# Scores for three pairs at a time in six PSUM banks, two accumulator banks that change hands by halves, and an earlier load of the second batch's v

## The chip, the cores and the metric

The kernel runs on one core of a Trainium2 chip. The metric is the time of one execution on the device, in microseconds (us); the time before is the median of three runs.

## The reference

Attention without softmax, multiplied by `u`, feeds a mixture of experts with one expert per token and a fixed capacity. `u` and `v` are 8 x 3072 x 256, `z` is 8 x 3072 x 64, there are 8 experts with 1024 hidden units, and the capacity is 768 tokens per expert.

```python
scores = (1 / S) * matmul(z, z.T)               # per batch, z is query and key
x = u * matmul(maximum(scores, 0) ** 2, v)      # flattened to tokens
expert = argmax(x @ w_gate); gate = softmax(x @ w_gate)[expert]
disp[e, pos] = x[i]                             # in order of tokens, while pos < capacity
y = maximum(disp @ w1, 0) @ w2
out[i] = gate[i] * y[expert[i], pos[i]]         # 0 for tokens over capacity
```

## The kernel before

Every operand of a matmul is split in a high and a low f16 half, and three products (high-high, high-low, low-high) are added in PSUM. Since experts fill up, the kernel computes attention for the first 14 blocks of 512 tokens only, and goes on in a part that is skipped unless some expert is not full.

**Attention.** A block of 512 queries meets 3072 keys as 12 pairs of 128-key tiles. For each pair, `team` makes scores on TensorE in 64-row matmuls, two side by side in the array (the two key tiles of the pair), 12 instructions for a team of two pairs; each pair takes two banks of the PSUM tag `sc`. `follow` then queues, for each pair, two ReLUs and a square on ScalarE and two passes on VectorE that make the f16 halves in a buffer with the tag `hl`. The main loop multiplies a pair by v: for each of four query tiles `c` six 128-row matmuls, 24 for a pair. The sums of a block stay in two banks of the tag `acc` (`c` = 0, 1 in one, 2, 3 in the other) over all 12 pairs, until `drain` multiplies a bank by `u` on VectorE. Scores are symmetric, so a block makes only part of its pairs: others are transposed out of DRAM (`kept`, loaded as `ld`) or straight from the block before (`nx`, and `corner` for one pair). The 14 blocks make 106 pairs, in 53 teams.

**Banks.** PSUM has eight banks: four for `sc`, three for `acc`, one for `m`, which holds the small products (router logits `lg`, running counts `cum`, and `fps`).

**Order.** The program's order is written by a planner: `op` keeps a model clock for each engine, a `Chain` is a list of steps that wait for engines, `weave` emits what fits beside the matmuls, and `need` moves the model clock of TensorE on until a step is there. Chains of lower rank go first; rank -1 are the followers of scores, -2 the drains. `scores_to(p + 3)` makes a team when the main loop is three pairs ahead of the team's first pair. `calm` keeps chains of rank above 0 off ScalarE and VectorE around the end of a block.

**Around it.** `prepare` loads and splits z and v of a batch of six blocks; for the second batch it is called at pair 12, and all its loads go through the queue of SyncE (SP), where kept blocks, transposes and u go too. `route` (GpSimd scatters its rows to DRAM) and then `ffn`, run for the 8 experts one after the other, follow. In `ffn` the hidden products use `sc` with four banks, the outputs `acc` with three.

Of the kernel before, what the change touches and what calls it, by code (L numbers as in the profile page):

```python
# [20 lines left out]
MROW = 8  # L21
BIG = 1 << 21
# [4 lines left out]
def attention_moe_kernel(ctx: ExitStack, tc: tile.TileContext, u, v, z, w_gate, w1, w2, out, cap):  # L27
# [148 lines left out]
    calm = [False]  # L176
    DMAROOM = 1.2
    chains = []
    done = {}
    small = [False]  # L180

# [19 lines left out]
    class Chain:  # L201
# [38 lines left out]
        def fits(self):  # L240
# [4 lines left out]
            if any(small[0] if k == "small" else k not in done or it[0] == "PE" and done[k] + 3.0 > now for k in it[4:]):  # L245
                return False
# [3 lines left out]
            if eng in ("ACT", "DVE"):  # L250
# [5 lines left out]
                if self.rank < 0:  # L256
                    return self.rank < -1 or ("pair", 3) in done or t - now <= 0.2
# [34 lines left out]
    def init_disp():  # L292
# [13 lines left out]
        def put():  # L306
# [4 lines left out]
              4, clk["PE"] + 1.0, gate="consts")  # L311
# [22 lines left out]
    def prepare(bt, first=False, swap=()):  # L334
# [12 lines left out]

        def ld_z(i):
            def f():
                if i == 0:  # L350
                    bt.zraw = sb.tile([P, JT, DQ], F32, tag="zraw", name="zraw", bufs=1)
                    bt.vm = sm.tile([P, NV + 2], F32, tag="vm", name="vm")
                    if first:
                        nc.vector.memset(bt.vm[:, NM:NM + 1], 2.0 ** -112)
# [7 lines left out]
        def ld_v(i):  # L362
            def f():
                t = sb.tile([P, 4, D], F32, tag="raw", name="vraw", bufs=6)
                nc.sync.dma_start(out=t, in_=vr[:, 4 * i:4 * i + 4, :])  # L365
                bt.vraw[i] = t
            return f
# [29 lines left out]
        def z_group(g):  # L397
# [15 lines left out]
            def tr():  # L413
                if g < 2:
                    st.tp = [ps.tile([P, 4, P], F16, tag="sc", name="ztp", bufs=4) for r in range(2)]
                else:
                    t = ps.tile([P, 2, 4, P], F16, tag="m", name="ztp", bufs=1)
# [4 lines left out]

            left = [2]

            def ev(r):
                def f():
# [3 lines left out]
                    left[0] -= 1  # L430
                    if g >= 2:
                        small[0] = left[0] > 0
# [3 lines left out]
                    [("PE", 0.45, tr, None) if g < 2 else ("PE", 0.45, tr, None, "small")],  # L436
# [122 lines left out]
        if not first:  # L559
            for i in range(zparts):  # L560
                Chain([[("SP", 4.4, ld_z(i), None)]] + norm(i), 1, slow=20.0)
            for i in range(NV):
                Chain([[("SP", 1.46, ld_v(i), None)], [mark(i)]], 2, slow=20.0)
# [15 lines left out]
        if not first:  # L579
# [3 lines left out]
                         lambda: Chain([[("DVE", 0.4, factor, key("f"))]], 3, max(done[key("v", 0)], done["gate"]))))  # L583
# [89 lines left out]
    def route(x, bt, after, lag, cc, rid, follows=(), ahead=(), snapped=()):  # L673
# [31 lines left out]
        def r_lg():  # L705
            st.lg = ps.tile([P, cc, 2, E], F32, tag="m", name="lg", bufs=1)
# [21 lines left out]
        def r_cum():  # L728
            st.cum = ps.tile([P, cc, E], F32, tag="m", name="cum", bufs=1)
# [57 lines left out]
        def tr(h):  # L787
# [8 lines left out]
            [("PE", 0.15, r_lg, None, "small")],  # L796
            [("DVE", 1.1, free(r_arg), None)],
            [("PE", 0.05, r_cum, None, "small") + follows, ("DVE", 0.1, r_dexp, None)],
# [5 lines left out]
    def counts(c=cnt):  # L804
        t = ps.tile([P, E], F32, tag="m", name="fps", bufs=1)
# [44 lines left out]
    def attention(blocks, hook):  # L850
# [3 lines left out]
        bank, held = [0], {}  # L854
        rids = []
# [46 lines left out]
        teams = deque(tuple(computed[i:i + 2]) for i in range(0, len(computed), 2))  # L902
        assert all(len(t) == 2 and t[1] == t[0] + 1 and t[0] % 2 == 0 for t in teams)
# [15 lines left out]
        def team(ps_):  # L919
# [3 lines left out]
            n, g = at(ps_[0])  # L923
            bt, ib, c0, cc = blocks[n]
            t = need(bt.key("z", 2 * g // 4), bt.key("z", ib))
            made = []
            for p in ps_:
                if place[p] >= 2:
                    t = max(t, need((aid, "r", place[p] - 2)))
# [3 lines left out]
                s = [ps.tile([P, BLK], F32, tag="sc", name="sc", bufs=4) for _ in range(2)]  # L933
# [5 lines left out]
                t = op("PE", 0.1 + 3 * w / 2400, t)  # L939
# [3 lines left out]
        def follow(p, s, w, t):  # L943
# [17 lines left out]
            def hi():  # L961
                hl = sb.tile([P, 2, nt, 2, HB], F16, tag="hl", name="hl", bufs=5)
# [29 lines left out]
            def keep():  # L992
# [4 lines left out]

            st = [[("ACT", 0.05 + w * 0.00084, relu(0), None), ("ACT", 0.05 + w * 0.00084, relu(1), (aid, "r", k))],
                  [("ACT", 0.09 + w * 0.00168, square, (aid, "s", k))],
                  [("DVE", 0.07 + w * 0.00107, hi, None, bt.key("vs")), ("DVE", 0.29 + w * 0.0021, lo, (aid, "a", p))]]  # L1000
# [6 lines left out]
            return Chain(st, -1, t, gate=(aid, "s", k - 1) if k else None, hold=HOLD)  # L1007

        def scores_to(p):
            while teams and teams[0][0] - (2 if cornered(teams[0][1]) and blocks[teams[0][0] // NPAIR][1] else 0) <= p:  # L1010
                team(teams.popleft())

# [34 lines left out]
        for p in range(NP):  # L1047
            n, g = at(p)
            bt, ib, c0, cc = blocks[n]
            hook(p)  # L1050
            done.setdefault(("pair", p), clk["PE"])
            loads_to(p + 4)
            i = p % NPAIR
            if i == 0:
                acc[n] = {}
            calm[0] = p < NP - 1 and (i == NPAIR - 1 or i == 0 and n > 0)
            if i == NPAIR // 2:
                ld_u(n)
            for c in range(cc):
                if c % (cc // 2) == 0:  # L1060
                    scores_to(p + 3 if p > 3 else p + 2 if p or c else 0)
                    weave()
# [379 lines left out]
```

## Time and profile before

| | us |
|---|---|
| median of three runs | 787.63 (786.09 to 788.51) |
| the profiled execution | 781.93 |
| its span, from first to last instruction | 780.2 |
| TensorE busy | 770.2 (99%) |
| VectorE busy | 515.7 (66%) |
| ScalarE busy | 400.9 (51%) |
| GpSimd busy | 120.4 (15%) |
| attention on TensorE | until 521.9 |
| experts on TensorE | from 521.9 to the end |

The profile is of one execution. A group of matmuls that overlap in the array is busy as a whole, so a busy TensorE says only that no gap was seen; whether the array streamed at its full rate is read from how many matmuls start in a stretch of time. A wait is put down to the engine or the transfer whose semaphore came last.

### The profile page before, as it was taken

Reading aid. Unit: us, or ns where it says so; the run is one execution under the profiler, and the core shown is the slowest. Engines: PE = TensorE matmul, PEld = TensorE weight load, DVE = VectorE, ACT = ScalarE, POOL = GpSimd, SP = SyncE. Lnnn points to the kernel's source line nnn. Section 1 sums busy time; section 2 is a strip of 40 time slices with the busy share of each in tenths; the row PEclk is TensorE's granted clock in tenths of the full one; section 3 lists DMA queues with packets and bytes.
Section 4 is the critical chain, followed back from the end, with each engine's and each line's share of the span. In section 5 each row is a group of like instructions: output and inputs, shape, how many; then the busy total and the mean of one; then the engine's idle time right before and its main releaser. Section 6 shows DMA issues by size and latency. Waiting matters only on the chain.

```text
span 780.2 us, 16284 instructions
## 1 busy us (share of the span) xinstructions
PE 770.2 (99%) x6474; PEld 569.7 (73%) x6474; DVE 515.7 (66%) x1134; ACT 400.9 (51%) x690; POOL 120.4 (15%) x122
## 2 busy tenths in 40 slices
PE   9999999999999999999999999999999999999996
PEld 3787878888887777878888877876666666666664
DVE  7996888853517789974553259889476575575741
ACT  6966545533206646663431048675455564464541
POOL 0000102020202010210202020202421321313202
PEclk9999999999999999999999999999999999999999
DMA  7659999999988949999969959970698945845001
GB/s 223 142 198 192 256 204 233 203 222 174 185 155 179 286 153 189 225 197 224 204 146 190 180 155 229 338 178 22 206 301 297 332 137 223 285 127 186 28 15 45
DMA packets 283830, 149.49 MB, mean 192 GB/s; under 512 B 229741, under 2 KB 255674, under 8 KB 283744
## 3 DMA queue, kind: packets, MB, share of 16 engines
q1 hardware_dynamic: 278848, 135.57, 71.7%
q0 software_dynamic: 4896, 12.79, 4.8%
q8 instruction: 52, 0.85, 0.5%
q14 instruction: 34, 0.28, 0.1%
HBM read 36.25 MB, written 59.92 MB: 123 GB/s over the span
## 4 chain that ended last, share of the span: by engine, by line
PE 84%; issue 5%; DMA 3%; DVE 2%; SPq 2%; POOL 2%; ACT 1%; POOLq 0%; ACTq 0%; DVEq 0%
PE acc L1083 52%; PE hps L1224 12%; PE yps L1248 11%; PE sc L937 8%; POOL out L84 1%; DMA vraw<-in_v 1%; DMA ld<-kept 1%; DMA wraw<-in_moe_w 1%; SPq L910 1%; PE lg L709 1%; SPq L365 1%; ACT a L959 0%; DVE hl L972 0%; DVE hh L1210 0%; DVE wt L1151 0%
## 5 line engine op out<-in xcount | busy, mean ns | idle before, releaser
L1083 PE MATMUL acc<-v,hl 128*128 128x256 f16 x2280 | 261.2, 273 | 0.2 <-DVE v L520 0.2
L1083 PEld LDWEIGHTS <-hl 128*128 128x128 f16 x2280 | 219.6, 98 | 34.7 <-issue 5.4
L954 ACT ACTIVATE r<-sc 128x512 f32<-128x512 f32 (+1 forms) x212 | 105.5, 550 | 164.8 <-PE sc L937 163.1
L1224 PE MATMUL hps<-fxt,wt 128*128 128x384 f16 (+2 forms) x816 | 127.5, 317 | 0.5 <-DVE hh L1210 0.5
L1248 PE MATMUL yps<-wt,hh 128*128 128x256 f16 (+1 forms) x776 | 126.6, 324 | 0.0
L972 DVE TENSOR_TENSOR hl<-a,hl 128x1024 f16<-128x1024 f32 (+1 forms) x106 | 118.2, 1115 | 3.6
L84 POOL DMA_INDIRECT disp<-xr,slot x54 | 60.6, 1122 | 378.2 <-issue 134.0
L1224 PEld LDWEIGHTS <-wt 128*128 128x128 f16 x816 | 77.5, 98 | 47.8 <-issue 0.9
L1248 PEld LDWEIGHTS <-hh 128*128 128x128 f16 x776 | 75.6, 98 | 48.6
L1083 PE MATMUL acc<-v,ld 128*128 128x256 f16 x960 | 109.2, 273 | 1.2 <-DMA ld<-kept 1.2
L959 ACT ACTIVATE a<-r 128x1024 f32<-128x1024 f32 (+1 forms) x106 | 102.6, 968 | 2.2
L1083 PEld LDWEIGHTS <-ld 128*128 128x128 f16 x960 | 93.0, 98 | 12.7 <-DMA ld<-kept 1.5
L963 DVE CAST hl<-a 128x1024 f16<-128x1024 f32 (+1 forms) x106 | 67.8, 639 | 50.0 <-ACT a L959 49.4
L1210 DVE SCALAR_TENSOR_TENSOR hh<-hps,hh 128x384 f16<-128x384 f32 (+2 forms) x136 | 70.7, 531 | 33.9 <-ACT hh L1209 33.4
L1209 ACT ACTIVATE hh<-hps 128x384 f16<-128x384 f32 (+2 forms) x136 | 63.4, 471 | 50.5 <-PE hps L1224 49.3
L84 POOL DMA_INDIRECT out<-ys,sid x48 | 53.3, 1111 | 126.5 <-DVE ys L1257 74.5
L937 PE MATMUL sc<-zz 64*128 64x512 f16 (+1 forms) x636 | 71.4, 356 | 0.4 <-DVE zz L427 0.2
L1254 ACT ACTIVATE ys<-yps,sg 128x256 f32<-128x256 f32 x48 | 22.6, 472 | 72.6 <-PE yps L1248 68.2
L1083 PE MATMUL acc<-v,nx 128*128 128x256 f16 x504 | 58.5, 273 | 0.0
L1257 DVE SCALAR_TENSOR_TENSOR ys<-yps,sg,ys 128x256 f32<-128x256 f32 x47 | 22.6, 483 | 51.9 <-ACT ys L1254 51.4
L1083 PEld LDWEIGHTS <-nx 128*128 128x128 f16 x504 | 48.4, 98 | 8.3 <-issue 2.8
L691 ACT ACTIVATE xr<-x,rsr 128x256 f16<-128x256 f32 x54 | 24.8, 501 | 55.4 <-DVE rsr L60 51.8
(135 smaller groups left out, 485.1 us busy)
## 6 DMA issues: line engine op xcount, KB each, us to landing
out<-zero SPq DMA_DIRECT2D x48, 512.0 KB, 9.0
kept<-hl SPq DMA_DIRECT2D x40, 512.0 KB, 4.8
wraw<-in_moe_w SPq DMA_DIRECT2D x32, 512.0 KB, 6.1
vraw<-in_v SPq DMA_DIRECT2D x18, 512.0 KB, 6.4
u<-in_u SPq DMA_DIRECT2D x13, 512.0 KB, 5.7
zraw<-in_z SPq DMA_DIRECT2D x2, 768.0 KB, 6.3
zz<-zz SPq DMA_DIRECT2D x4, 384.0 KB, 4.6
xt<-xr SPq DMA_TRANSPOSE x54, 2.5
```

The lines of the kernel that those rows point to most:

```text
L84: r = nc.gpsimd.indirect_dma_start(out=dst, out_offset=bass.IndirectOffsetOnAxis(ap=idx, axis=0), in_=src, in_offset=None, bounds_check=bo ...
L691: return lambda: nc.scalar.activation(st.x16[:, c, 0:D], st.x[:, c, :], AF.Copy, scale=st.rs[:, c:c + 1])
L937: nc.tensor.matmul(s[jj][:, 0:w], lhsT=bt.zz[rows, (kl + jj) % 2, j * P:(j + 1) * P], rhs=bt.zz[rows, (ql + jj) % 2, q0:q0 + w], start=(i ...
L954: nc.scalar.activation(sct[p][:, jj, :], s[jj][:, 0:w], AF.Relu)
L959: nc.scalar.activation(sq[p], sct.pop(p), AF.Square)
L963: nc.vector.tensor_copy(hl[:, :, :, 0, :], sq[p].rearrange("p j (t k) -> p j t k", k=HB))
L972: nc.vector.tensor_sub(hl[:, :, :, 1, :], a.rearrange("p j (t k) -> p j t k", k=HB), hl[:, :, :, 0, :])
L1083: nc.tensor.matmul(o, lhsT=a(h, jj, c), rhs=bt.v2[:, j, l], start=(i + jj + h + l + c % 2 == 0), stop=(i == NPAIR - 1 and jj + h == 2), sk ...
L1209: Chain([[("ACT", 0.05 + w * 0.00083, lambda: nc.scalar.activation(th, src, AF.Relu), None)], [("DVE", 0.07 + w * 0.00104, lambda: nc.vect ...
L1210: [("DVE", 0.07 + w * 0.00104, lambda: nc.vector.scalar_tensor_tensor(out=tl, in0=src, scalar=0.0, in1=th, op0=ALU.max, op1=ALU.subtract), ...
L1224: nc.tensor.matmul(o, lhsT=wx.w1[:, d, wp, f * P:(f + 1) * P], rhs=sx.xt[:, xp * DC + d, a:a + w], start=(q == 0), stop=(q == len(seq) - 1))
L1248: nc.tensor.matmul(y[:, 0 if end else l], lhsT=hid(i, f)[:, sl], rhs=w[:, l], start=(f + i == 0 and l != 1), stop=(f == FC - 1 and i == 1) ...
```

## The change

- Teams of the opening (the first six pairs) stay as they are; all later ones take three computed pairs (`TEAM = 3`), in six `sc` banks. A team may hold pairs on either side of stored pairs or of a block's end.
- The `m` bank is gone: `ztp`, `lg`, `cum` and `fps` take a bank of `sc`. `open_bank` lets a small product in only when the bank it takes has been read, and at least four query tiles before the next team is due; `team` holds TensorE's place in the order until the small product has been read.
- `acc` has two banks. At a block's start and end two pairs are taken together: both for `c` = 0, 1, then both for `c` = 2, 3 (`steps`). `turning` keeps followers of scores from being queued ahead there.
- In `ffn` both kinds of products share the six `sc` banks.
- `hl` has six buffers instead of five, and its VectorE pass is emitted only once the buffer is through (`room_for`); `corner` has a buffer of its own.
- The second batch's v is loaded from pair 3 on, one load for every two pairs, each after the first batch's v in its buffer has been split; z still starts at pair 12.
- The scratch space for dynamic DMA is 8192 instead of the default, and a few ranks and one delay of the third expert's weights change.

```diff
+NHL = 6
+TEAM = 3
-        t = ps.tile([P, BLK], F32, tag="acc", name="warm", bufs=3)
+        t = ps.tile([P, BLK], F32, tag="acc", name="warm", bufs=2)
...
+            if "small" in it[4:] and self.ready + self.lag <= now and not clear[0]():
+                return False
...
-                    return self.rank < -1 or ("pair", 3) in done or t - now <= 0.2
+                    return self.rank < -1 or ("pair", 3) in done and not turning[0] or t - now <= 0.2
...
-                    t = ps.tile([P, 2, 4, P], F16, tag="m", name="ztp", bufs=1)
+                    t = ps.tile([P, 2, 4, P], F16, tag="sc", name="ztp", bufs=6)
...
             for i in range(NV):
-                Chain([[("SP", 1.46, ld_v(i), None)], [mark(i)]], 2, slow=20.0)
+                Chain([[("SP", 1.46, ld_v(i), None) + (held(i) if held else ())],
+                       [mark(i) + ((("pair", NPAIR + 1 + i),) if held else ())]], 2, slow=20.0)
...
-            st.lg = ps.tile([P, cc, 2, E], F32, tag="m", name="lg", bufs=1)
+            st.lg = ps.tile([P, cc, 2, E], F32, tag="sc", name="lg", bufs=6)
...
-        teams = deque(tuple(computed[i:i + 2]) for i in range(0, len(computed), 2))
+        opening = hasattr(blocks[0][0], "to_scores")
+        k = 6 if opening else 0
+        teams = deque(tuple(computed[i:i + 2]) for i in range(0, k, 2))
+        teams.extend(tuple(computed[i:i + TEAM]) for i in range(k, len(computed), TEAM))
...
+            while small[0]:
+                weave()
+                clk["PE"] += 0.1 if small[0] else 0.0
+            latest[:] = [0, *((aid, "r", place[p]) for p in ps_)]
...
-                if place[p] >= 2:
-                    t = max(t, need((aid, "r", place[p] - 2)))
+                if place[p] >= TEAM:
+                    t = max(t, need((aid, "r", place[p] - TEAM)))
-                s = [ps.tile([P, BLK], F32, tag="sc", name="sc", bufs=4) for _ in range(2)]
+                s = [ps.tile([P, BLK], F32, tag="sc", name="sc", bufs=6) for _ in range(2)]
...
-                        corner[n] = sb.tile([P, 4, HB], F16, tag="ld", name="corner", bufs=5)
+                        corner[n] = sb.tile([P, 4, HB], F16, tag="corner", name="corner", bufs=1)
...
+            def room_for():
+                return k < NHL or computed[k - NHL] in through and lines[k - NHL].item() is None
...
+        def open_bank():
+            p, c = where
+            if latest:
+                k = latest[1 + min(latest[0] // 2, len(latest) - 2)]
+                if k not in done or done[k] + HOP > clk["PE"]:
+                    return False
+            if teams and (due() - 3 - p) * CC - c < 4:
+                return False
...
+        def steps():
+            for n, (_, _, _, cc) in enumerate(blocks):
+                i = 0
+                while i < NPAIR:
+                    both = cc == CC and (i == 0 and not (opening and n == 0) or i == NPAIR - 2)
+                    for h in range(2 if both else 1):
+                        for j in range(2 if both else 1):
+                            for c in (2 * h, 2 * h + 1) if both else range(cc):
...
+                                turning[0] = both and (i > 0 or n > 0 and h + j < 2)
+                                yield n * NPAIR + i + j, c
+                    i += 2 if both else 1
...
-                    k = bank[0] - 3
+                k = bank[0] - 2
-                    acc[n][c // 2] = ps.tile([P, 2, D], F32, tag="acc", name="acc", bufs=3)
+                acc[n][c // 2] = ps.tile([P, 2, D], F32, tag="acc", name="acc", bufs=2)
...
-                h = ps.tile([P, BLK], F32, tag="sc", name="hps", bufs=4)
+                h = ps.tile([P, BLK], F32, tag="sc", name="hps", bufs=6)
-            y = ps.tile([P, 2, D], F32, tag="acc", name="yps", bufs=3)
+            y = ps.tile([P, 2, D], F32, tag="sc", name="yps", bufs=6)
...
-            if g == 0 and ib == (b == 0) and b + 1 in bats:
+            if p == 1 and 1 in bats:
+                prepare(bats[1], swap=(("pair", 3 * NPAIR + 3),),
+                        held=lambda i: (b0.key("v", 2 * i + 1), ("pair", 2 * i + 3)))
+            if p == NPAIR and 1 in bats:
+                bats[1].begin_z()
+            if p == b * BPB * NPAIR and b and b + 1 in bats:
                 prepare(bats[b + 1], swap=(("pair", p + 2 * NPAIR + 3),))
...
-    nc = _bacc.Bacc("TRN2", target_bir_lowering=False, num_devices=1)
+    nc = _bacc.Bacc("TRN2", target_bir_lowering=False, num_devices=1, dynamic_dma_scratch_size=8192)
```

## Rows read from the trace of the kernel before

**Rows 1.** The page: busy time and instructions of TensorE, and its 40 slices.

```profile
PE 770.2 (99%) x6474; PEld 569.7 (73%) x6474; DVE 515.7 (66%) x1134; ACT 400.9 (51%) x690; POOL 120.4 (15%) x122
PE   9999999999999999999999999999999999999996
```

**Rows 2.** Waits of TensorE, whole span: us in total, times, longest us.

```profile
PE acc L1083 <- DMA ld<-kept: 1.2, 1, 1.2
PE warm L151 <- DVE ones L121: 1.1, 1, 1.1
PE hps L1224 <- DVE hh L1210: 0.5, 2, 0.4
```

**Rows 3.** Chain that ended last, pieces in order: start us, us, what.

```profile
107.22 1.40 PE sc L937 x12
108.62 5.34 PE acc L1083 x48
113.96 1.40 PE sc L937 x12
...
127.98 1.08 PE sc L937 x12
129.06 15.83 PE acc L1083 x144
...
309.20 2.64 PE acc L1083 x24
...
511.19 0.76 PE sc L937 x12
```

**Rows 4.** Timeline of TensorE, 95 to 110 us, around the one wait for a transfer.

```profile
101.80 2.79 PE L1083 MATMUL acc<-v,ld 128*128 128x256 f16 x24 [1.22 <-DMA ld<-kept]
```

**Rows 5.** Timeline of the SP queue, 80 to 102 us: start us, us of issue.

```profile
84.35 0.53 SPq L365 DMA_DIRECT2D vraw<-in_v  x1
...
86.67 6.25 SPq L910 DMA_TRANSPOSE ld<-kept  x1
92.96 0.58 SPq L365 DMA_DIRECT2D vraw<-in_v  x1
93.58 4.52 SPq L910 DMA_TRANSPOSE ld<-kept  x1
...
99.56 0.94 SPq L365 DMA_DIRECT2D vraw<-in_v  x1
```

**Rows 6.** Stretches: busy us of each engine, granted clock, DMA share, GB/s.

```profile
30.00:60.00 30.00, 30.00 (x273) 23.45 (x271) 27.18 (x52) 22.34 (x35) 0.35 (x1) 1.00 0.75 205
...
80.00:100.00 20.00, 20.00 (x202) 16.39 (x200) 16.42 (x35) 9.24 (x15) 4.87 (x4) 1.00 1.08 271
```

**Rows 7.** Groups by line and shape, ScalarE and VectorE: busy us, mean ns, idle before.

```profile
L954 ACT ACTIVATE r<-sc 128x512 f32<-128x512 f32 x168 | 91.0, 594 | 159.0 <-PE sc L937 157.9
L959 ACT ACTIVATE a<-r 128x1024 f32<-128x1024 f32 x84 | 88.7, 1056 | 1.6
```

**Rows 8.** Line of the drains: duration min/median/max ns; idle of VectorE before them.

```profile
L1025 DVE TENSOR_TENSOR x<-acc,u x27: 678/692/692, 57.5 to 522.1; 128x512 f32<-128x512 f32 x27
...
  PE acc L1083: 23.2, 19
```

**Rows 9.** Timeline of VectorE, ends of block 5 (241 us) and block 11 (463 us).

```profile
241.25 0.69 DVE L1025 TENSOR_TENSOR x<-acc,u 128x512 f32<-128x512 f32 x1 [3.04 <-PE acc L1083]
241.86 0.69 DVE L963 CAST hl<-a 128x1024 f16<-128x1024 f32 x1
242.58 1.23 DVE L972 TENSOR_TENSOR hl<-a,hl 128x1024 f16<-128x1024 f32 x1
243.72 0.69 DVE L963 CAST hl<-a 128x1024 f16<-128x1024 f32 x1
244.44 1.23 DVE L972 TENSOR_TENSOR hl<-a,hl 128x1024 f16<-128x1024 f32 x1
245.58 0.69 DVE L1025 TENSOR_TENSOR x<-acc,u 128x512 f32<-128x512 f32 x1
...
462.77 0.69 DVE L1025 TENSOR_TENSOR x<-acc,u 128x512 f32<-128x512 f32 x1 [3.04 <-PE acc L1083]
...
467.11 0.68 DVE L1025 TENSOR_TENSOR x<-acc,u 128x512 f32<-128x512 f32 x1
```

**Rows 10.** Timeline of TensorE in the experts, 564 to 580 us.

```profile
566.35 1.50 PE L1224 MATMUL hps<-fxt,wt 128*128 128x128 f16 x24 [0.35 <-DVE hh L1210]
...
576.51 2.11 PE L1224 MATMUL hps<-fxt,wt 128*128 128x384 f16 x12 [0.16 <-DVE hh L1210]
```

**Rows 11.** DMA issues of the whole span: KB each, median us to landing.

```profile
vraw<-in_v SPq DMA_DIRECT2D x18, 512.0 KB, 6.4
...
disp<-xr,slot POOLq DMA_INDIRECT x54, 3.9
```

**Rows 12.** A slice of experts: line's DMA to landing (min/median/max), SP's issue, TensorE's use.

```profile
DMA to landing us min/median/max: 3.2/5.1/11.4
...
552.99 1.19 SPq L1178 DMA_TRANSPOSE fxt<-disp  x1
...
564.49 1.50 PE L1224 MATMUL hps<-fxt,wt 128*128 128x128 f16 x24
```

**Rows 13.** Timeline of GpSimd, 541 to 554 us: the densest run of scatters.

```profile
540.95 1.17 POOL L84 DMA_INDIRECT disp<-xr,slot  x1 [22.70 <-DVE ys L1257]
...
552.73 0.97 POOL L84 DMA_INDIRECT out<-ys,sid  x1 [0.31 <-issue]
```

More of the change, by code (lines that the diff above doesn't have):

```diff
@@ L176, in attention_moe_kernel @@
     calm = [False]
+    turning = [False]
     DMAROOM = 1.2
@@ L180, in attention_moe_kernel @@
     small = [False]
+    clear = [lambda: True]
     def free(fn):
@@ L244, in fits @@
             now = clk["PE"]
-            if any(small[0] if k == "small" else k not in done or it[0] == "PE" and done[k] + 3.0 > now for k in it[4:]):
+            if any(small[0] if k == "small" else not k() if callable(k) else
+                   k not in done or it[0] == "PE" and done[k] + 3.0 > now for k in it[4:]):
+                return False
+            if "small" in it[4:] and self.ready + self.lag <= now and not clear[0]():
                 return False
@@ L332, in batch, with prepare @@
         return bt
-    def prepare(bt, first=False, swap=()):
+    def prepare(bt, first=False, swap=(), held=None):
         zparts = 3 if first else 1
@@ L365, in f @@
                 nc.sync.dma_start(out=t, in_=vr[:, 4 * i:4 * i + 4, :])
+                if not bt.vraw and not first:
+                    new_max()
                 bt.vraw[i] = t
@@ L854, in attention @@
         bank, held = [0], {}
+        where, latest, lines, through = [0, 0], [], {}, set()
         rids = []
@@ L1046, in attention @@
             scores_to(0)
[L1047 removed]
+        clear[0] = open_bank
+        operand = {}
+        for p, c in steps():
+            where[:] = p, c
             n, g = at(p)
             bt, ib, c0, cc = blocks[n]
[L1050 to L1052 removed]
             i = p % NPAIR
[L1054 to L1062, printed above, removed]
[L1063 to L1089 removed]
@@ new lines, in attention @@
+            if c == 0:
+                hook(p)
+                done.setdefault(("pair", p), clk["PE"])
+                loads_to(p + 4)
+                if i == 0:
+                    acc[n] = {}
+                if i == NPAIR // 2:
+                    ld_u(n)
+            if c % (cc // 2) == 0:
+                scores_to(p + 3 if p > 3 else p + 2 if p or c else 0)
+                weave()
+            if c == 0:
+                if is_next(p):
+                    take(p)
+                clk["PE"] = max(clk["PE"], need((aid, "a", p), bt.key("v", g),
+                                                *([(aid, "d", n)] if cornered(p) else [])) + HOP)
+                operand[p] = prs.pop(p)
@@ new lines, in attention @@
+            a = operand[p]
+            if i == 0 and c % 2 == 0:
+                k = bank[0] - 2
+                if k in held:
+                    clk["PE"] = max(clk["PE"], need((aid, "x", *held[k])) + HOP)
+                held[bank[0]] = n, c // 2
+                bank[0] += 1
+                acc[n][c // 2] = ps.tile([P, 2, D], F32, tag="acc", name="acc", bufs=2)
+            o = acc[n][c // 2][:, c % 2]
+            for jj in (0, 1):
+                j = 2 * g + jj
+                for h, l in ((0, 0), (0, 1), (1, 0)):
+                    nc.tensor.matmul(o, lhsT=a(h, jj, c), rhs=bt.v2[:, j, l], start=(i + jj + h + l + c % 2 == 0),
+                                     stop=(i == NPAIR - 1 and jj + h == 2), skip_group_check=True)
+                op("PE", 0.328, 0.0)
+                weave()
@@ L1090, in attention @@
+            if i == NPAIR - 1 and c % 2:
+                drain(n, c // 2)
+            if c == cc - 1:
+                through.add(p)
+                operand.pop(p)
+            if i == NPAIR - 1 and c == cc - 1:
+                calm[0] = False
                 need(bt.key("f"), "init")
@@ L1303, in experts @@
                 wxs[i + 1] = Bag()
-                weights(es[i + 1], wxs[i + 1], gate=((eid, "through", i - 1),) if i else ())
+                weights(es[i + 1], wxs[i + 1], gate=((eid, "through", i - 1),) if i else (), slow=5.0 if i == 1 else 0.0)
             if straight[0] and k > 0:
```

95 lines of the change are left out of this document (42 added, 53 removed).

## The prediction

> **What bounds the kernel now.** I read the page first: TensorE is busy for 770.2 of 780.2 us, and VectorE, the next, for 515.7 [rows 1]. Next come TensorE's waits: the longest is 1.2 us for a stored block, the experts wait 0.5 us in two places for VectorE, and with a start of 1.1 us these are nearly all [rows 2]. So hardly any stall is left to remove; the time is what TensorE issues. A busy array is not yet one that streams at its full rate, so the third view is the chain that ended last, read as a clock. In a stretch without scores, 144 matmuls of 256 columns take 15.83 us, 0.1099 us each [rows 3]. The granted clock is 1.00, the 2.4 GHz level, in every stretch read [rows 6], so no gain can come from the clock either.
>
> The same rows show what a team of scores costs beyond its columns. A team of two pairs, both 512 wide, takes 1.40 us; with one pair of 256 it takes 1.08, and with both at 256 it takes 0.76 [rows 3]. Each halved pair takes off 0.32 us, which is three streams of 256 columns at 0.107 us. Six streams of 512 columns are then 1.28 us, and 0.12 us of each team is a fixed cost. From one team to the next, with 48 matmuls between, it is 113.96 - 107.22 = 6.74 us; 48 x 0.1099 + 1.28 = 6.56, so a team costs 0.18 us in all, partly before and partly after it. I use 0.18 to 0.19. It is paid when the array goes from 128-row to 64-row matmuls and back, once for a team, however many pairs it holds.
>
> **Part by part.**
>
> Teams of three. There are 106 pairs made, 53 teams before. After, the opening keeps 3 teams for 6 pairs, and the other 100 pairs make 33 teams of three and one of one: 37 in all. 16 teams fewer x 0.19 us = -3.0 us (-2.9 by the lower value). All of it lies on TensorE, which ends the time, so nothing hides it. Matmuls, columns and weight loads stay the same.
>
> What a team of three asks of ScalarE: two ReLUs of 0.594 us and a square of 1.056 for a pair [rows 7], 2.24 us, 6.7 us for the team. A team needs all six banks, so the last pair's second ReLU must be done before the next team. It ends some 0.64 + 2 x 2.24 + 1.19 = 6.3 us after the team began (0.64 us are the first pair's columns); the next team begins after 1.92 + 0.19 us of scores and 72 matmuls, 10.0 us after this one. So 3.7 us are left for other work of ScalarE (before: 0.64 + 2.24 + 1.19 = 4.1 of 6.74, 2.6 left). I take 0 for this wait. A pair's halves are needed no sooner than before, since the team still comes three pairs ahead, and the second and third have longer.
>
> Two accumulators. A drain takes 0.69 us, and 19 of 27 ran the moment their bank was complete, with VectorE idle before them [rows 8]. After, the other bank is worked on for 24 matmuls, 2.64 us [rows 3], before a drained bank is wanted. So a drain may start 1.95 us late and cost nothing. With three banks one of the two drains of a block already had just this window, and no wait for it shows [rows 2]; the other had a whole block. At the end of block 5 that other drain started at 245.58, behind two pairs' conversions [rows 9]; its bank was complete 1.32 us (12 matmuls) after the first drain's, at 242.57, so it ended 3.70 us after that. In the new order this would cost 3.70 - 2.64 = 1.06 us. At the end of block 11 the drain ran as late [rows 9]: bank complete at 462.77 + 1.32, drained by 467.79. `turning` lets at most one such pass of VectorE (1.23 us) go ahead of a drain, and that fits in the 1.95. The bounds are 0 and 13 boundaries x 1.06 = 13.8 us; I take 0.8 us, less than one late boundary, because nearly all rows are on the side of on time.
>
> Here a rule stands against the change. The Trainium skill, in Perfetto Trace Analysis, section Matmuls under Optimizing Tensor Performance, wants independent matmul groups to rotate through PSUM banks so that the evacuation of one overlaps the next group. Read strictly, a block's two banks are both its own, no third bank covers the drain, and 26 drains x 0.69 = 17.9 us would lie open. The row of 2.64 us speaks against that reading, since the halves let each bank cover the other; the rule's case is the slower rival below.
>
> The small products (14 `lg`, 14 `cum`) lose their bank. They are admitted after the first ReLUs of a team and at least four query tiles (2.64 us) before the next; the window is some 5 of every 10 us. Their instructions stay the same, and a team waits only if VectorE hasn't read the bank. Bounds: 0, and 28 reads behind one 1.23 us pass, 34 us; I take 0, since VectorE is a third idle and the first reader is at the head of its chain. Delay of the router itself ends in scatters that the experts want only at 522 us; nothing on TensorE waits for them earlier.
>
> The early v. TensorE's one wait for a transfer is at 101.80, 1.22 us, for a stored block [rows 4]. That transfer's issue stood on the SP queue from 93.58 to 98.10, behind another that took 6.25 us and two loads of v [rows 5]. DMA is full there (share 1.08, 271 GB/s), and has room in 30 to 60 us (0.75, 205 GB/s) [rows 6]. A load of v is 512 KB; at 205 to 271 GB/s that is 2.0 to 2.6 us each. The two loads of the rows and one more at 99.56 leave this place, so the stored block comes some 4 to 5 us earlier. It is also wanted earlier: 1.32 us by the new order of the first two pairs, and 0.6 us by the three teams saved until then. 1.22 + 1.32 + 0.6 = 3.1 us, under 4; so the wait should go, -1.2 us, but with little to spare: bounds -1.2 and +1.9. In exchange some five loads, 10 to 13 us of DMA, enter 30 to 68 us; what is queued behind them on SP there are writes of `kept` and transposes for the next block, not wanted before 59 us. The maxima of v stay on VectorE, held to block 1, so VectorE's full start (27 of 30 us [rows 6]) gets no more to do. I take -1.0.
>
> Six banks for the experts. Two waits of 0.35 and 0.16 us are for a hidden bank still read by VectorE [rows 10]; with six banks instead of four both should go: -0.5 us. Outputs come from the same six; a bank is wanted again five products later, far longer than the reads take.
>
> Answers at nothing: six `hl` buffers, a buffer for `corner` (leaves five for stored blocks alone), ranks, and the later third weights take away waits or move work that is off TensorE; `room_for` holds a pass back in the order rather than in VectorE's queue.
>
> The sum: -3.0 - 1.0 - 0.5 + 0.8 = -3.7 us. On the profiled execution's 781.93 us that gives 778.2. That execution is 5.7 us under the median of the runs shown; I carry the difference over unchanged, so 787.63 - 3.7 = 783.9 us, 0.47% faster. A measurement of this kernel can tell about 0.3%, 2.4 us, from no change.
>
> **The rivals.**
>
> What is late before stays late. The drains of blocks 5 and 11 cost 2 x 1.06 = 2.1 us in place of my 0.8, and the stored block is waited for as before, 0 in place of -1.0: -3.0 - 0.5 + 2.1 = -1.4, 786.2 us, no change to be told. For it: the halves put two drains where conversions already stood, and the stored block has less than 1 us to spare by my sum. Against it: `turning`, and the two loads that stood in front of it are gone.
>
> Slower: every boundary waits for its drain. A drain that is queued behind two pairs' conversions, as at block 5 [rows 9], costs 1.06 us; at 13 boundaries 13.8 us. With -4.5 us from the other terms that is 796.9. It decides against the change from 0.35 us a boundary on, and is slower to be told from 0.53. For it: block 5 shows the order; against it: 19 of 27 drains on time.
>
> Fewer scatter slots: the change sets the scratch space of dynamic DMA to 8192 in place of its default. The Trainium skill, in SBUF — State Buffer, section on SBUF size, sets 16 KiB of a partition aside for the descriptor rings of GpSimd's DMAs; by that the rings are halved, and no row here shows how full they get. The densest run is ten scatters between 540.95 and 553.70, one every 1.28 us [rows 13], while a landing takes 3.9 us [rows 11], so three are in the air. If each had to wait for the last, these ten would take 39 us instead of 12.8, 26 more. The experts' slice that follows was issued at 552.99 and first used at 564.49, and its landing takes 5.1 us [rows 12], so 6.4 us are to spare and some 20 would be waited: 787.6 - 3.7 + 20 = 804. Against it: the rings as they are show no wait at three in the air, and room for just one would be a far greater cut than a smaller scratch suggests.
>
> The change doesn't do what it says: teams are made late or the moved loads move the wait to another stored block. Only the saved switches less 1 to 2 us are left, about 786 us; it counts with the first rival.
>
> **How the numbers follow.** The forecast, all terms near their value: 0.60. First rival and the like: 0.24. Late drains everywhere: 0.12. Scatters: 0.04. The forecast's cases lie within 781.5 (-3.0 - 1.2 - 0.5 with no new wait is 782.9, and runs spread by over 1 us) and 785.2. The range goes on through the first rival and a few late boundaries to 789.5; over that lies most of the slower cases, under 781.5 little. Faster by over 0.3%: 0.60; within: 0.26; slower: 0.14.
>
> **What would show it.** After: 38 stretches of `sc` on TensorE instead of 54 (the second team of the opening is in two parts), full ones of 18 matmuls lasting 2.04 us (1.92 + 0.12); no wait for `ld` near 100 us; no wait of `hps` for `hh`. Wrong would be the prediction if TensorE waited for a drain (`x`) or for a ReLU at `sc`, if stretches between teams fell short of 0.110 us a matmul, or if scatters came further apart than 1.28 us in the dense run.

## The result, and the profile after

The changed kernel takes 778.47 us (median of 6 runs, 776.74 to 779.68), the kernel before 787.26 us beside it on the same chip (6 runs, 786.09 to 788.51). The ratio is 0.9886, 95% interval 0.9872 to 0.9900: 8.8 us faster, where 3.7 were forecast, and 3 us under the low end of the range. The profiled execution of after took 778.41 us, span 776.5, so it stands in the middle of its runs. That of before did not, and this turns out to be the point of the case.

TensorE on the page of after, beside [rows 1], and its waits, beside [rows 2] (us in total, times, longest us):

```profile
PE 766.8 (99%) x6474; PEld 572.3 (74%) x6474; DVE 514.4 (66%) x1134; ACT 401.1 (52%) x690; POOL 116.6 (15%) x122
...
PE warm L153 <- DVE ones L123: 1.1, 1, 1.1
PE acc L1141 <- DVE v L527: 0.6, 2, 0.5
PE acc L1141 <- DMA ld<-kept: 0.6, 2, 0.3
PE ztp L433 <- DVE zhl L422: 0.5, 2, 0.3
PE acc L1141 <- DVE wm L1188: 0.3, 1, 0.3
```

No wait for a drain (`x`), none for a ReLU at `sc`, none of `hps` for `hh`. The wait for a stored block has fallen from 1.2 us to two that come to 0.6. Without the start, `warm`, the four kinds of small waits come to 2.0 us; those for `ztp` and `wm` are new beside [rows 2].

The chain of after, pieces in order (start us, us, what), beside [rows 3]:

```profile
32.21 2.05 PE sc L958 x18
34.26 5.35 PE acc L1141 x48
39.61 2.05 PE sc L958 x18
41.66 7.96 PE acc L1141 x72
49.62 1.73 PE sc L958 x18
```

A team of three takes 2.05 us: 1.92 of columns and 0.13. From 39.61 to 49.62 it is 10.01 us for a team and 72 matmuls of 0.1099 us: 10.01 - 7.91 - 1.92 = 0.18 us for the team, as much as a team of two cost. There are 38 stretches of `sc` in the whole trace.

If one sets this trace beside the profile of before that stands in the front, attention is 2.4 us shorter (its last matmul starts at 521.82 and 519.38) and the rest 1.3 us: 3.7 us of span, just what I forecast. But the runs differ by 8.8. So 5 us are not in the trace of before at all, and the first thing to do was to profile that kernel again.

### The profile page after: what moved, and what is told of

It is laid out like the page before. It is cut to its first block, busy times and chain, and to the rows that moved or that the text cites. A ratio compares the mean times of both kernels' runs of the same rounds, so it can differ in the third digit from the quotient of the medians.

```text
span 776.5 us, 16291 instructions
## 1 busy us (share of the span) xinstructions
PE 766.8 (99%) x6474; PEld 572.3 (74%) x6474; DVE 514.4 (66%) x1134; ACT 401.1 (52%) x690; POOL 116.6 (15%) x122
## 4 chain that ended last, share of the span: by engine, by line
PE 88%; issue 3%; DMA 3%; DVE 2%; POOL 1%; SPq 1%; ACT 0%; POOLq 0%; ACTq 0%; DVEq 0%
PE acc L1141 51%; PE hps L1287 14%; PE yps L1311 14%; PE sc L958 8%; DMA ld<-kept 2%; DMA vraw<-in_v 1%; POOL out L86 1%; PE lg L722 1%; DVE hl L993 1%; SPq L375 0%; DVE hl L984 0%; DVE wm L75 0%; DVE xr L707 0%; DVE v L527 0%; SPq L369 0%
## 5 line engine op out<-in xcount | busy, mean ns | idle before, releaser
L86 POOL DMA_INDIRECT disp<-xr,slot x54 | 56.8, 1051 | 359.7 <-issue 215.5
L958 PE MATMUL sc<-zz 64*128 64x512 f16 (+1 forms) x636 | 68.5, 355 | 0.0
```

Of the source, the lines that this page charges most:

```text
L86: r = nc.gpsimd.indirect_dma_start(out=dst, out_offset=bass.IndirectOffsetOnAxis(ap=idx, axis=0), in_=src, in_offset=None, bounds_check=bo ...
L958: nc.tensor.matmul(s[jj][:, 0:w], lhsT=bt.zz[rows, (kl + jj) % 2, j * P:(j + 1) * P], rhs=bt.zz[rows, (ql + jj) % 2, q0:q0 + w], start=(i ...
```

## Experiments

**The kernel before once more** (`ctl`, nothing edited).

> The kernel before, unchanged. Open: its runs take 787.3 us, the profiled execution took 781.93. Theory A (a wait that comes and goes): this profile has a span near 785.5 and TensorE has about 5 us of waits that the first profile has not, most of them for transfers. Theory B (the extra lies outside the span): the span is again 780 and the time 787. Against the kernel before: ratio 1.000 within 0.002.

Its median is 787.98 us beside 788.03 for the same kernel, ratio 0.9999 [0.9985, 1.0012], and its profiled execution took 787.93 us, span 786.1, in the middle of the runs. Theory A is right that a wait is there, and wrong about its kind: it is for VectorE and not for a transfer. Waits of TensorE, then TensorE around the second slice of the experts (640 rows are the first slice, 384 and 128 the second and third):

```profile
PE hps L1224 <- DVE hh L1210: 3.6, 2, 3.5
...
548.28 4.07 PE L1224 MATMUL hps<-fxt,wt 128*128 128x384 f16 x24
555.80 6.80 PE L1224 MATMUL hps<-fxt,wt 128*128 128x384 f16 x24 [3.46 <-DVE hh L1210]
562.44 7.96 PE L1248 MATMUL yps<-wt,hh 128*128 128x512 f16 x48
```

The first 24 matmuls (four banks of hidden values) take 4.07 us, then TensorE waits 3.46 us for a bank, and the next 24 take 6.80. ScalarE, which has to read those banks, shows that VectorE is only the last in a row (idle time before an instruction in brackets):

```profile
546.11 0.47 ACT L1254 ACTIVATE ys<-yps,sg 128x256 f32<-128x256 f32 x1 [2.36 <-PE yps L1248]
551.87 0.47 ACT L1254 ACTIVATE ys<-yps,sg 128x256 f32<-128x256 f32 x1 [5.28 <-PE hps L1224]
554.67 1.64 ACT L1209 ACTIVATE hh<-hps 128x384 f16<-128x384 f32 x4 [2.33 <-remote]
```

The output that ScalarE scales at 551.87 was complete when the first slice's last matmul ended, some 0.2 us after 548.28; the four ReLUs at 554.67 came all at once. So ScalarE sat idle beside finished work for 3.4 of the 5.28 us, and for all of the 2.33. Meanwhile GpSimd issued ten scatters (first and last of the row, 1.28 us apart, 0.30 between them):

```profile
540.33 1.16 POOL L84 DMA_INDIRECT disp<-xr,slot  x1 [22.27 <-DVE ys L1257]
...
552.09 0.97 POOL L84 DMA_INDIRECT out<-ys,sid  x1 [0.30 <-issue]
```

And the windows (length; busy us of PE, PEld, DVE, ACT, POOL; granted clock; DMA share; GB/s):

```profile
552.00:556.00 4.00, 0.54 (x4) 0.20 (x2) 1.29 (x3) 1.67 (x5) 0.97 (x1) 0.82 0.55 116
556.00:562.00 6.00, 6.00 (x22) 2.93 (x21) 2.26 (x5) 1.63 (x4) 0.97 (x1) 0.55 0.97 328
```

After the pause the granted clock is 0.55, near the 1.2 GHz level, so the stall is paid for once more: 24 matmuls take 6.80 us in place of 4.07, 2.7 us. Divided by place, ctl against after, in us of the two traces:

| Part of the span | ctl | after | after - ctl |
|---|---|---|---|
| up to the last matmul of attention | 521.22 | 519.38 | -1.84 |
| from there to the experts' second slice | 27.06 | 26.66 | -0.40 |
| second and third slices | 27.36 | 20.93 | -6.43 |
| from the fourth to the last outputs | 203.06 | 202.71 | -0.35 |
| behind them | 7.4 | 6.8 | -0.6 |

The 6.43 us are the stall and its clock. The last line is no part of the change: it varies from 6.6 to 7.9 us among the traces of this study, whatever the kernel. The first profile of before has 21.42 us in the second and third slices. The first line isn't exact either: in six traces in which the code of attention is that of before, its last matmul starts between 521.00 and 524.76, and in five traces with that of the change between 518.60 and 520.85.

**Are the switches and the moved v worth what I said?** `team2` is the change with teams of two; `vlate` is the change with the second batch's v loaded at pair 12 as before.

```diff
-TEAM = 3
+TEAM = 2
```
```diff
-            if p == 1 and 1 in bats:
-                prepare(bats[1], swap=(("pair", 3 * NPAIR + 3),),
-                        held=lambda i: (b0.key("v", 2 * i + 1), ("pair", 2 * i + 3)))
             if p == NPAIR and 1 in bats:
-                bats[1].begin_z()
+                prepare(bats[1], swap=(("pair", 3 * NPAIR + 3),))
```

> The change with teams of two pairs (TEAM = 2); banks, order by halves, early v and all else as in the change. Theory switches: 16 more teams at 0.19 us, 3.0 us over the change, 781.5 us against 787.3 of before (ratio 0.9926); 54 stretches of sc. Rival (the three-pair team itself frees VectorE or ScalarE from waits): the whole gain of 8.8 us goes, 787.

> The change with the second batch's v loaded from pair 12 on, as before; all else as in the change. Theory early v pays: the stored block near 100 us is waited for again, 1.2 us if the first profile is typical (779.7 us), 5 to 6 us if this is the wait that comes and goes (784). Rival (the early load pays nothing): 778.5, no wait of TensorE for ld near 100 us.

team2: 783.05 us (781.50 to 785.42), ratio 0.9941 [0.9921, 0.9961], 4.6 us over the change's median (4.3 by the two ratios; the two were taken on different occasions), where 3.0 were expected. From the first score to the end of attention its trace has 3.1 us more than that of after, 0.5 of it in more waiting, which leaves 2.6 for the switches; 16 teams x 0.18 are 2.9 us. The other 1.5 us of the medians are not in attention; 0.8 of them stand behind the last outputs, where any two traces differ.

vlate: 786.94 us (784.53 to 790.79), ratio 0.9994 [0.9978, 1.0010]; the whole gain is gone, 8.5 us, more than either value that was expected. TensorE waits for stored blocks twice, and the window behind it shows the clock:

```profile
98.89 1.48 PE L1141 MATMUL acc<-v,ld 128*128 128x256 f16 x12 [1.73 <-DMA ld<-kept]
105.00 6.44 PE L1141 MATMUL acc<-v,ld 128*128 128x256 f16 x36 [4.63 <-DMA ld<-kept]
...
105.00:112.00 7.00, 7.00 (x43) 5.40 (x44) 3.85 (x3) 0.00 (x0) 0.00 (x0) 0.66 0.58 127
```

The SP queue says why: in vlate four loads of v issued from 81.47 on, of which the last two are shown, stand ahead of the first transpose, which is issued at 88.59 for 7.44 us; in after the same place has none.

```profile
85.36 1.42 SPq L375 DMA_DIRECT2D vraw<-in_v  x2
...
88.59 7.44 SPq L926 DMA_TRANSPOSE ld<-kept  x1
...
97.59 4.45 SPq L926 DMA_TRANSPOSE ld<-kept  x1
```

The same two issues in after:

```profile
82.96 5.12 SPq L926 DMA_TRANSPOSE ld<-kept  x1
...
89.27 4.41 SPq L926 DMA_TRANSPOSE ld<-kept  x1
```

So 6.36 us of waiting and about 2.3 us of low clock (36 matmuls in 6.44 us; in team2 36 of the same kind take 4.10) stand against the 8.5 us of the medians.

**The moved v alone** (`vearly`: before, with v of the second batch loaded early and nothing else; the edit is that of the change to `prepare` and its calls, so the lines taken from vlate are put into before).

> The kernel before with the early load of the second batch's v alone. Theory early v pays: 1.2 us (786) by the first profile, 5 to 6 us (782) if the wait for the stored block is what comes and goes. Rival (pays nothing): 787.3, ratio 1.000.

788.92 us (786.73 to 790.42), ratio 1.0013 [1.0000, 1.0025]: worth nothing alone. No wait for a stored block is left, but there isn't always one to lose (with the same attention ctl lists none, scr8 0.9 us and hps6 1.4), and a wait of 1.12 us for a ReLU at 113.95 has come. The edits of this change don't add up: moving v is worth 8.5 us where the new order needs its stored blocks earlier, and 0 where it doesn't.

**What is it in the second slice: the banks, the weights, the scratch?** Three single parts put into before, and one taken out of the change. `hps6` gives hidden products seven banks in before, four of `sc` and three of `acc`; `slow5` delays the third expert's weights; `scr8` halves the scratch; `hps4` is the change with two of its six banks passed over after every four hidden products.

```diff
-                h = ps.tile([P, BLK], F32, tag="sc", name="hps", bufs=4)
+                h = ps.tile([P, BLK], F32, tag="sc" if k % 3 else "acc", name="hps", bufs=4 if k % 3 else 3)
```
```diff
...
-                weights(es[i + 1], wxs[i + 1], gate=((eid, "through", i - 1),) if i else ())
+                weights(es[i + 1], wxs[i + 1], gate=((eid, "through", i - 1),) if i else (), slow=5.0 if i == 1 else 0.0)
```
```diff
-    nc = _bacc.Bacc("TRN2", target_bir_lowering=False, num_devices=1)
+    nc = _bacc.Bacc("TRN2", target_bir_lowering=False, num_devices=1, dynamic_dma_scratch_size=8192)
```
```diff
+                if k % 4 == 1 and k > 1:
+                    for _ in range(2):
+                        ps.tile([P, BLK], F32, tag="sc", name="skip", bufs=6)
```

> The kernel before; in the experts every third hidden product takes an acc bank instead of an sc bank, so that a hidden bank is wanted again six products later instead of four, and nothing else. Theory banks (the wait of 3.5 us at 552 us in the second slice, and the clock that falls after it, 6.4 us in all, come from four hidden banks): 787.3 - 5 to 6.4, 781 to 782.5 us, no wait of hps of over 1 us. Rival (banks don't matter, ScalarE is late by more than two banks cover, or another part of the change took the wait away): 787.3 within 1 us.

> The kernel before with the delay of 5 us for the third expert's weights and nothing else. Theory order (ScalarE and VectorE stand behind the third expert's weights in the second slice): 781 to 782.5 us. Rival: 787.3 within 1 us, the wait at 552 us stays.

> The kernel before with the scratch space of dynamic DMA at 8192 and nothing else. If the smaller scratch made scatters wait: slower than 787.3 and scatters further apart than 1.28 us at 541 to 554 us. If it has no part in the gain: 787.3 within 1 us, and the wait at 552 us stays.

> The change with only four of the six banks for hidden products (two are passed over after every four), all else as in the change. Theory banks: the wait in the second slice comes back, 778.5 + 3 to 6.4 us. Rival (the change moved scatters and weights away from there, so four banks are enough): 778.5 within 1 us.

The kernel before took 788.88 us on this chip (23 runs).

| Kernel | Median us | Ratio | Second and third slices, us |
|---|---|---|---|
| hps6 | 784.26 | 0.9945 [0.9932, 0.9959] | 22.90 |
| slow5 | 789.29 | 1.0006 [0.9993, 1.0019] | 28.35 |
| scr8 | 788.42 | 0.9995 [0.9985, 1.0006] | 27.65 |
| hps4 | 778.62 | 0.9865 [0.9847, 0.9882] | 20.93 |

In before, the weights and the scratch play no part: the stall stays, and so does the time. More banks alone give 4.6 us back to before, between the values of the two theories, but hps4 does without them and loses nothing. Both hold if banks only cover the lateness and the change keeps it away from the hidden products. In hps6 it is still there, TensorE just meets it later and for less (this profiled execution is the slowest of its six, 787.16 us where the others took 783.58 to 784.47, so how much is left in a typical one isn't shown):

```profile
551.72 5.20 PE L1224 MATMUL hps<-fxt,wt 128*128 128x384 f16 x31
557.64 0.48 PE L1224 MATMUL hps<-fxt,wt 128*128 128x384 f16 x2 [0.72 <-issue]
...
559.57 2.11 PE L1224 MATMUL hps<-fxt,wt 128*128 128x384 f16 x12 [0.54 <-DVE hh L1210]
```

How late ScalarE is can be measured in every trace, from the end of the last matmul of a product to the start of the ScalarE instruction that reads it; on time is 0.04 us. Over the first slice's outputs and the second slice's hidden products the longest is 5.3 us in ctl, 5.2 to 5.6 in vearly, hps6, slow5 and scr8. The change isn't free of it. In after the first output, complete at 535.61, is taken up at 537.70, 2.1 us late, and the trace names nothing on this core that released it:

```profile
532.65 0.81 PE L1311 MATMUL yps<-wt,hh 128*128 128x512 f16 x4
533.50 2.11 PE L1311 MATMUL yps<-wt,hh 128*128 128x512 f16 x12
...
537.70 0.47 ACT L1317 ACTIVATE ys<-yps,sg 128x256 f32<-128x256 f32 x1 [3.86 <-remote]
```

The longest in hps4, vlate, after2 and noslow is 1.5 to 1.7 us, again at the first outputs, and TensorE waits for none of these. The hidden products of the second slice are at most 0.35 us late in after and 0.8 in hps4.

What the change does differently there is seen on GpSimd in after:

```profile
536.50 0.97 POOL L86 DMA_INDIRECT disp<-xr,slot  x1 [0.30 <-issue]
538.97 0.97 POOL L86 DMA_INDIRECT out<-ys,sid  x1 [1.49 <-DVE p L780]
542.04 1.12 POOL L86 DMA_INDIRECT disp<-xr,slot  x1 [2.11 <-ACT ys L1317]
...
547.36 0.97 POOL L86 DMA_INDIRECT out<-ys,sid  x1 [0.30 <-issue]
```

The small products of the last full block run earlier (its `cum` at 525.35, in ctl at 533.93), so its four scatters lie between 532.62 and 537.5, and the ten that were one row in ctl are four, one and five with pauses of 1.49 and 2.11 us. No run puts this earlier place of the small products into before alone.

**The scatters taken out and put back.** `noys` is before without the five output scatters of the first slice, so those rows of the result are not written. `dump` is the change with six scatters more in the same stretch: the rows of the last two blocks are also written to a part of DRAM that nothing reads.

```diff
-lambda t=t: scatter("out", out, tid[:, t:t + 1], ys[t], NTOK - 1)
+lambda t=t: n == 640 or scatter("out", out, tid[:, t:t + 1], ys[t], NTOK - 1)
```
```diff
...
-            [("POOL", 1.04, r_sc(c), (rid, "sc", c)) + ahead for c in range(cc)],
+            [("POOL", 1.04, r_sc(c), (rid, "sc", c)) + ahead for c in range(cc)] +
+            ([("POOL", 1.04, r_dump(c), None) for c in range(cc)] if ahead else []),
```

> The kernel before, with the scatters of the first slice's five outputs left out (those rows of the result are not written); all else is as before. In the traces of before that take 787 us, TensorE's results between 548 and 555 us are told up to 3.5 us late, while GpSimd makes ten scatters in a row from 540 to 553. Theory scatters (results are told late while scatters follow each other without a pause): with four of the ten gone the row ends near 548, results are on time from about 549.5, the wait of hps falls from 3.5-4 to under 1 us, 781 to 783 us. Rival (this place of the program is late for another reason): wait and time stay, 787 to 788.

> The change, with six more scatters behind those of the last two blocks: the same rows go once more to DRAM that nothing reads. Theory scatters: rows of eight to ten scatters as in before, TensorE's results are told late again somewhere between 535 and 556, a wait of 1 to 6 us with a fall of the clock, 780 to 785 us. Rival (scatters have no part): 778.5 within 1 us.

noys: 782.89 us (781.14 to 783.87) beside 786.99, ratio 0.9960 [0.9947, 0.9973]. The stall is gone: second and third slices take 21.01 us.

```profile
548.06 7.96 PE L1224 MATMUL hps<-fxt,wt 128*128 128x384 f16 x48
555.86 7.96 PE L1248 MATMUL yps<-wt,hh 128*128 128x512 f16 x48
...
546.80 0.97 POOL L84 DMA_INDIRECT disp<-xr,slot  x1 [0.30 <-issue]
561.16 0.97 POOL L84 DMA_INDIRECT out<-ys,sid  x1 [13.39 <-DMA out<-zero]
```

ScalarE is at most 0.6 us late there. The gain of 4.1 us by the medians, 3.1 by the ratio, is less than the 6.4 between the traces of ctl and after; the profiled execution of noys was the quickest of its six, and its chip ran before 1 us quicker than that of ctl.

dump: 788.36 us (785.58 to 791.90), ratio 1.0022 [1.0005, 1.0038], 9.9 us over the change and over the 780 to 785 expected. GpSimd issues 15 scatters without a pause (first and last), ScalarE takes up an output as much as 10.7 us late, and TensorE itself falters; the window has the clock behind it:

```profile
532.03 1.03 POOL L86 DMA_INDIRECT disp<-xr,slot  x1 [14.16 <-ACT wt L1219]
...
550.63 0.97 POOL L86 DMA_INDIRECT out<-ys,sid  x1 [0.30 <-DVE ys L1329]
...
549.47 0.84 PE L1296 MATMUL hps<-fxt,wt 128*128 128x384 f16 x2
551.40 0.48 PE L1296 MATMUL hps<-fxt,wt 128*128 128x384 f16 x1 [1.09 <-issue]
...
555.00:560.00 5.00, 5.00 (x19) 2.42 (x18) 1.60 (x4) 1.20 (x3) 0.89 (x1) 0.57 1.01 332
```

Attention ends at 518.78, 0.6 us earlier than in after, and the part from the fourth slice takes 202.71 us as there; all of the loss lies in the three slices between, 4.0 and 6.6 us. So fewer scatters take the loss away from before, and more in a row bring one to the change. Both runs also change how many scatters there are; neither shows what the pauses alone are worth.

It is not a rule without exceptions. The first profile of before has the same ten scatters 1.28 us apart [rows 13] and no lateness, and in team2 ten follow each other from 538.23 to 552.2 with no pause over 0.33 us, ScalarE is at most 0.25 us late, and the second and third slices take 21.00 us:

```profile
538.23 1.02 POOL L86 DMA_INDIRECT disp<-xr,slot  x1 [22.33 <-DVE sid L1297]
...
551.24 0.97 POOL L86 DMA_INDIRECT out<-ys,sid  x1 [0.30 <-issue]
...
549.06 7.96 PE L1287 MATMUL hps<-fxt,wt 128*128 128x384 f16 x48
```

In team2 three of the ten last 1.36 to 1.51 us; in the first profile of before none does. Since team2 is the change but for the size of its teams, and its execution lies in the middle of its runs, splitting the row can't be all that frees the change of the stall. Why these two executions escape isn't shown.

One rival that no run tests is the recording itself. A trace notes the updates of semaphores, the counters by which an instruction or a transfer tells that it is done. For each of the ten scatters of [rows 13] the first trace of before holds 16 such updates, and in all 10004; ctl, the same program, holds 2 to 7 for nine of its ten and 9011 in all, and no trace but the first holds more than 9133. So the execution that was 5 us quicker is also the only one whose record has no gaps there. Records are missing from noys and team2 as well, which have no stall, so missing records alone don't make one; whether the writing of them does, together with the scatters, is open.

**The change again, and without its delay** (`after2`, `noslow`).

```diff
-weights(es[i + 1], wxs[i + 1], gate=((eid, "through", i - 1),) if i else (), slow=5.0 if i == 1 else 0.0)
+weights(es[i + 1], wxs[i + 1], gate=((eid, "through", i - 1),) if i else ())
```

> The change once more, unchanged: the spread of its runs, and a second trace. 778.5 within 1 us of median; by the theory of scatters no wait of hps over 0.5 us.

> The change without the delay of 5 us for the third expert's weights. Theory: no part in the gain, 778.5 within 1 us. Rival: ScalarE stands behind the weights in the third slice and hps or yps wait, 779.5 to 781.

after2: 777.81 us (777.42 to 783.90), ratio 0.9913 [0.9887, 0.9939]; four of its six runs lie within 0.5 us, the others took 780.62 and 783.90, and no trace shows where these lost the time. noslow: 777.59 us (776.04 to 781.12), ratio 0.9895 [0.9874, 0.9916]. The change's median holds when measured again, and the delay of the third expert's weights does nothing there either; 0.2 us can't be told.

## Why the prediction was wrong

**The step that failed** is the last of the sum: that execution "is 5.7 us under the median of the runs shown; I carry the difference over unchanged". Carried over unchanged it had to be something that both kernels pay outside what I was changing. It wasn't. Of the 76 other runs of before, on four occasions, and ctl's twelve, none came under 784.68 us; the profiled 781.93 was an execution apart. What it lacked sits in one place, the second slice of the experts (second and third slices: 27.36 us in ctl, 26.09 to 28.35 in vearly, scr8 and slow5 too, 21.42 there), and the change does away with it (20.93 to 21.00 in after, after2, noslow, hps4, vlate and team2). The sum by a typical trace is -2.9 for switches, +1.3 for small waits (2.0 us against 0.7 in ctl, both without the start, and ctl's without the stall), about 0 for early v, -6.4 for the second and third slices and -0.75 for the rest of the experts: -8.8 us, and the runs give -8.8. That the numbers meet to the tenth is luck; the same code of attention differs by up to 3.8 us among the traces.

**The term that was mis-sized** with it: "six banks for the experts -0.5", from two waits of 0.35 and 0.16 us [rows 10]. The wait for `hh` that these rows show in small is 3.6 us in ctl, and 6.4 with its clock. The banks are also not what ends it: hps4 lacks them and keeps the gain. For the small waits themselves the term was about right: from the fourth slice on, where no trace has the stall, hps4 takes 203.15 us and after 202.71. What the runs show in place of the banks is that the stall hangs on GpSimd's scatters: four fewer end it in before (noys), six more bring one to the change (dump). That the change escapes by moving them apart, through small products let in earlier, is likely and not shown; team2 escapes with its ten in one row. I had written of them that nothing on TensorE waits for the router's scatters before 522 us; I looked for who needs the scatters' data, and not for what else goes with a row of scatters.

**Switches, right.** -3.0 forecast; the cost of a team is 0.18 us before and after, and 38 stretches of `sc`, full ones of 2.05 us, were forecast as 38 and 2.04. team2 puts 2.6 us back in attention beside its waits.

**Early v, right in direction and wrong as a term by itself.** -1.0 forecast, the wait for `ld` down from 1.2 to 0.6 us in these two traces. But vearly alone is worth 0 and vlate costs 8.5. My margin (3.1 us of need, 4 to 5 of gain) was for the new order, and rightly close: in the trace of hps4 1.9 us of it are still waited for. I priced keeping the old place at +1.9 us at the worst; it is 8.5: 6.36 us of waiting at two transposes behind loads of v, and 2.3 for the lower clock after it.

**Two accumulators, right in the main.** +0.8 was taken for late drains and none is waited for, in after or in the six other traces with two accumulators; with three, vearly, hps6, slow5 and scr8 each wait 0.5 to 0.7 us for one. The 27 drains still take 0.69 us. The Trainium skill, in Perfetto Trace Analysis, section Matmuls under Optimizing Tensor Performance, wants groups to rotate through banks so that the evacuation of one overlaps the next group. That rule holds here with just two banks, because the halves give each drain 2.64 us of the other bank's matmuls; the reading by which 26 drains lie open doesn't. The small waits that did come (for `v`, `ld`, `ztp` and `wm`) are no drains; they happen to add 1.3 us where 0.8 were taken.

**The rivals.** Slower by late drains: TensorE waits for none. Scatter slots: the scratch space that the Trainium skill, in SBUF — State Buffer, section on SBUF size, sets aside plays no part at half its size, as scr8 shows in before: ratio 0.9995, scatters 1.28 us apart as ever. The change with the default scratch wasn't tried. What is late before stays late: no. None of the rivals was the one that came: a stall of before that its profile didn't show.

**The range** reached 781.5 at the low end because each case lay within the rows of one trace. I had the warning in hand: the profiled execution was 4 us under the lowest of the runs shown, and they spread by 2.4 us. A distance larger than the spread is no offset to be relied on, and the range should have reached down by the 5.7 us, to 776.

**What stays open:** by what path finished results are taken up late while scatters are issued, and TensorE itself falters in dump; why two profiled executions with such a row don't show it; what in the change, besides or in place of the split row, keeps the lateness from the hidden products; and whether the recording has a part. The runs settle where the missing 5 us lie, that fewer scatters take the stall out of before, and that more bring one to the change.

## What to carry to other kernels

Set the profiled execution beside the other runs before any sum: where it lies outside their spread, the difference can be a stall at one place that the trace in hand doesn't have, and a change near that place can win or lose all of it. Profile that kernel again first. Price a moved load in the new order as well as in the old; an edit that is worth nothing alone can be what holds another one up. And when looking for a stall's cause, look at GpSimd's densest run of scatters even where nobody waits for their data.

## What was not expected of the hardware

- A row of ten indirect scatters, 0.97 us each and 0.30 apart, went, in five traces of seven, with ScalarE taking up finished results of TensorE 3.4 us late and more (in ctl 551.87 for a product complete at 548.44). With 15 in a row TensorE's own matmuls come with gaps of 0.2 to 1.1 us for which the trace shows no wait. Split in rows of four, one and five, as in after, the longest delay is 2.1 us and holds up nothing.
- A pause of TensorE of 3.5 to 4.6 us was followed by a granted clock of 0.55 to 0.66 over the next 6 to 7 us, and cost 2.3 to 2.7 us beside the pause itself: 24 matmuls of 384 columns in 6.80 us in place of 4.07, 36 of 256 in 6.44 in place of 4.10.
